# A recurrent attention kernel: the mask matmul cut to the columns of the last keys, the token-token mask moved to a multiply on GpSimd

## The chip, the cores and the metric

The kernel runs on one core of a Trainium2 chip. The metric is the device time of one execution in microseconds; a kernel is timed several times, alternating with the kernel before on the same chip, and medians of its runs are given. Engines are named as the profile names them: PE (TensorE), DVE (VectorE), ACT (ScalarE), POOL (GpSimd).

## The reference, cut to what matters

A memory-augmented attention walks over a sequence of 2048 tokens in 64 segments of 32 tokens. Each segment's input is 8 memory rows and its 32 tokens; the output of the memory rows is the memory of the next segment, so the segments follow each other strictly. The result is mixed with an MLP by a gate.

```python
L = M + seg_len                                    # 8 + 32
mask = (idx[:, None] < M) | (idx[:, None] >= idx[None, :])   # memory rows see all, tokens are causal
for s in range(n_seg):                             # 64
    h = jnp.concatenate([mem, xs], axis=1)
    # q, k, v of 32 heads of 128
    scores = jnp.einsum('bhqe,bhke->bhqk', q, k) * scale
    scores = jnp.where(mask[None, None], scores, -1000000000.0)
    p = _softmax(scores, axis=-1)
    # o = p v, projected by Wo
    mem = o[:, :M, :].copy()
```

## The kernel before

One segment's scores stand in one PSUM bank as 8 groups of 56 columns (EW = 56). E holds their exponentials, R the reciprocals of the sums over the keys. Pm is E times R for the memory rows, on the path to the next segment; Px is the same for the tokens, and racc adds up R for a check against overflow. Keys are on the partitions. Columns 8 to 47 of a group are 24 + 8 tokens and 8 memory rows against the main keys; columns 0 to 7 and 48 to 55 are queries against the last 8 keys (LEFT) of several segments, which are computed ahead and need a selecting mask. The mask is put in first, as a matmul of an identity with a mask tile of 448 columns; the scores are added on top.

```python
def mask_mm():
    B = bank(7, [P, 512])
    S = B[:, 0:NG * EW].rearrange("p (i e) -> p i e", e=EW)
    nc.tensor.matmul(S, lhsT=ident[:], rhs=MkA[:].unsqueeze(2).to_broadcast([P, 4, 2, EW]),
                     start=True, stop=True, skip_group_check=True)
    return B, S
...
for s in range(nseg + 2):
    ...
    if si == 3 and T + 1 < NT:
        left_v_in(T + 1)              # POOL: copy VL, 128 x 1024
    if si == 3 and T + 2 < NT:
        x_left(T + 2)                 # POOL: copy GL
    if live:
        ...
        if s + 1 < nseg:
            prep_h(s + 1)             # POOL: copy part of hT
        if s >= 1:
            prep_q(s)                 # POOL: copy part of QT
            x_mul(s - 1)              # POOL: products Px, and racc += R
        flush(dve_q)
        ...                           # projections, scores into S
        nc.scalar.activation(out=E[:, :, 0:16], in_=S[:, :, 0:16], func=ACTF.Exp, ...)
        nc.scalar.activation(out=E[:, :, 16:EW], in_=S[:, :, 16:EW], func=ACTF.Exp, ...)
        sm = bank(nc_, [P, NG, 8])    # sums over the keys, for the memory rows
        nc.tensor.matmul(sm[:], lhsT=BO[:], rhs=E[:, :, 8:16], start=True, stop=False)
        nc.tensor.matmul(sm[:], lhsT=BO[:], rhs=E[:, :, 0:8], start=False, stop=True)
        run_fill(5 + (si == 3))       # PE: independent matmuls of other segments
        nc.vector.reciprocal(out=R[:, 0:8 * NG]..., in_=sm[:])
        nc.vector.tensor_tensor(out=Pm[:]..., in0=E[:, :, 0:16]..., in1=R[:, 0:8 * NG]..., op=ALU.mult)
        av(Um, 8, s, V, Pm, 8, 0, 0)  # PE: Pm times V
        nc.tensor.matmul(sr, lhsT=BO[:], rhs=E[:, :, 16:48], start=True, ...)   # sums for the tokens
        ...
```

Four segments make a tile T of 128 tokens, si is the number within it. The copies at the head of a segment are independent of what runs there, and POOL, which works in order, does them early: those written at the head of segment s run during segment s - 1.

## Time and profile before

| what | value | where from |
|---|---|---|
| time | 851.37 us | median of 3 runs, 849.81 to 851.44 |
| PE busy | 96% of the span | page, part 1 |
| recurrent loop | 120 to 838 us, 64 segments of 11.2 us | busy time by stretches |
| mask matmul in the chain | 0.29 us a segment | chain in order of time |
| Pm beside an idle POOL | 0.29 us | timeline |

The chain in order of time is read as a list of pieces: the start, the length, and the engine and line whose work was the last to end there. The timeline gives every engine's instructions, also those off the chain. In the loop one PE matmul stream fills nearly all the time, so the questions to ask of a change are what it takes from PE and what PE will wait for. The lines themselves are in the prediction.

### The profile page before, as it was taken

The page shows a single profiled execution, that of the slowest core. Times are in us where ns is not written, and L with a number is a line of the kernel's source. Part 1 is how long each engine was busy: PE and PEld are TensorE (multiplying, and loading weights), DVE is VectorE, ACT ScalarE, POOL GpSimd, SP SyncE. Part 2 cuts the span into 40 slices and gives each one's busy share as a digit, 9 for nine tenths or more (in the row PEclk, how much of TensorE's full clock was granted, in tenths as well). Part 3 has the DMA queues.
Part 4 walks back from the last instruction along what each step waited for, and adds up shares of the span by engine and source line. Part 5 has one row for each costly group of instructions (what it writes and reads, how often), then busy time and mean ns, then how long its engine had stood idle before and what let it go on. Part 6 is the DMA issues. An engine that isn't in the chain of part 4 may idle for free.

```text
span 848.8 us, 49249 instructions
## 1 busy us (share of the span) xinstructions
PE 813.2 (96%) x22417; PEld 495.7 (58%) x22417; DVE 502.4 (59%) x1017; ACT 434.2 (51%) x1244; POOL 275.2 (32%) x625
## 2 busy tenths in 40 slices
PE   4989999999999999999999999999999999999986
PEld 2655455566656666556666665656665666656554
DVE  4555335666665666565666566666656566657553
ACT  2444454555545554555455555555454545555552
POOL 8000123333233424242424342333324342424220
PEclk8999999999999999999999999999999999999999
DMA  9890221010101010101000000101010101010000
GB/s 317 268 361 8 65 63 27 4 35 4 35 10 35 4 34 12 34 12 30 15 22 24 19 26 17 29 10 35 10 35 7 34 9 36 9 31 9 10 4 24
DMA packets 38216, 37.64 MB, mean 44 GB/s; under 512 B 13545, under 2 KB 36434, under 8 KB 36466
## 3 DMA queue, kind: packets, MB, share of 16 engines
q1 hardware_dynamic: 37874, 34.31, 12.3%
q8 instruction: 177, 2.90, 1.4%
q14 instruction: 37, 0.30, 0.1%
q0 software_dynamic: 128, 0.13, 0.1%
HBM read 26.03 MB, written 6.29 MB: 38 GB/s over the span
## 4 chain that ended last, share of the span: by engine, by line
PE 90%; DVE 6%; issue 1%; DMA 1%; SPq 1%; ACT 1%; DVEq 0%; ACTq 0%
PE b L210 34%; PE b L232 17%; PE b L221 17%; PE b L383 5%; PE hp L454 3%; PE bp L471 3%; PE b L359 2%; PE b L368 2%; PE b L660 1%; PE b L695 1%; PE b L388 1%; PE b L649 1%; DVE st L401 1%; DVE junk L422 1%; DMA Wo_sb<-in_A_x_dram 1%
## 5 line engine op out<-in xcount | busy, mean ns | idle before, releaser
L216 DVE STREAM_TRANSPOSE Tt<-b 128x512 f32<-128x512 f32 (+1 forms) x384 | 225.6, 613 | 79.1 <-PE b L210 65.4
L210 PEld LDWEIGHTS <-hT 128*32 128x32 bf16 x5120 | 134.8, 97 | 100.0 <-DVE hT L696 15.7
L232 PE MATMUL b<-Wo_sb,UTT 128*32 128x256 bf16 (+1 forms) x4736 | 162.7, 285 | 1.2 <-ACT UTT L595 0.8
L221 PE MATMUL b<-Wv_sb,hT 128*32 128x512 bf16 x2048 | 141.9, 378 | 0.0
L210 PE MATMUL b<-Wq_sb,hT 128*32 128x512 bf16 x2048 | 133.0, 379 | 1.4 <-DVE hT L696 1.4
L210 PE MATMUL b<-Wk_sb,hT 128*32 128x256 bf16 (+1 forms) x3072 | 133.4, 308 | 0.0
L232 PEld LDWEIGHTS <-UTT 128*32 128x32 bf16 x4736 | 121.3, 97 | 19.6 <-ACT UTT L595 1.5
L630 ACT CAST KT<-Tt 128x256 bf16<-128x256 f32 (+1 forms) x192 | 87.1, 476 | 53.6 <-DVE Tt L216 53.5
L581 POOL TENSOR_TENSOR Px<-E,R 128x256 bf16<-128x256 bf16 x64 | 43.1, 673 | 219.0 <-DVE R L665 219.0
L665 DVE RECIPROCAL R<-b 128x256 f32<-128x256 f32 x64 | 112.5, 1757 | 0.0
L630 POOL CAST QT<-Tt 128x512 bf16<-128x512 f32 x64 | 39.3, 614 | 192.3 <-DVE Tt L216 192.3
L595 ACT CAST UTT<-b 128x256 bf16<-128x256 f32 x256 | 76.8, 386 | 23.6 <-PE b L388 23.1
L684 ACT CAST wsb<-b 128x256 bf16<-128x256 f32 x66 | 24.6, 373 | 120.0 <-PE b L232 120.0
L653 DVE RECIPROCAL R<-b 128x64 f32<-128x64 f32 x64 | 35.6, 557 | 79.1 <-PE b L650 79.1
L630 ACT CAST QT<-Tt 128x512 bf16<-128x512 f32 x64 | 39.6, 619 | 67.6 <-DVE Tt L216 67.6
L459 ACT ACTIVATE hg<-hp,b_sb 128x256 bf16<-128x256 f32 x80 | 37.6, 473 | 54.1 <-PE hp L454 54.1
L383 PEld LDWEIGHTS <-V 32*128 32x128 bf16 x4096 | 35.2, 91 | 46.5 <-DVE Pm L655 32.4
L221 PEld LDWEIGHTS <-hT 128*32 128x32 bf16 x2048 | 49.5, 96 | 21.1
L664 ACT CAST UTT<-b 128x64 bf16<-128x64 f32 x128 | 20.9, 215 | 75.6 <-PE b L388 75.6
L454 PE MATMUL hp<-yT,w_sb 128*128 128x256 bf16 (+1 forms) x352 | 55.8, 284 | 2.5 <-DVE yT L444 2.5
L583 POOL TENSOR_TENSOR racc<-racc,R 128x320 f32<-128x320 f32 x64 | 55.6, 868 | 0.0
L471 PE MATMUL bp<-w_sb,hg 128*128 128x512 bf16 x160 | 50.0, 392 | 3.7 <-DVE c_all L474 3.7
(116 smaller groups left out, 1046.5 us busy)
## 6 DMA issues: line engine op xcount, KB each, us to landing
Wv_sb<-in_A_Wv_dram SPq DMA_DIRECT2D x4, 1024.0 KB
Wq_sb<-in_A_Wq_dram SPq DMA_DIRECT2D x4, 1024.0 KB
Wk_sb<-in_A_Wk_dram SPq DMA_DIRECT2D x4, 1024.0 KB
Wo_sb<-in_A_Wo_dram SPq DMA_DIRECT2D x2, 2048.0 KB
vd<-vt SPq DMA_DIRECT2D x32, 128.0 KB
vs<-vd SPq DMA_DIRECT2D x256, 16.0 KB
out_dram<-o SPq DMA_DIRECT2D x16, 128.0 KB
Wo_sb<-in_A_x_dram SPq DMA_DIRECT2D x1, 1024.0 KB
```

What stands on the lines that cost most here:

```text
L210: nc.tensor.matmul(bk[32 * j:32 * j + 32, 0:n], lhsT=G[:, kc, :], rhs=W5[t][:, kc, h0:h1, j, :], start=(kc == 0), stop=(kc == KC - 1), til ...
L216: nc.vector.transpose(out=Tt[:, 0:n], in_=bk[:, 0:n])
L221: nc.tensor.matmul(bk[32 * j:32 * j + 32, :], lhsT=G[:, kc, :], rhs=Wv5[:, kc, 4 * vb:4 * vb + 4, j, :], start=(kc == 0), stop=(kc == KC - ...
L232: nc.tensor.matmul(bk[32 * g:32 * g + 32, :], lhsT=ut[:, i, j, c0:c0 + 32], rhs=Wo_sb[:, 4 * i + j, d0:d1], start=(j == 0 and i < 4), stop ...
L383: nc.tensor.matmul(U[j][:, i, :], lhsT=V[q, i, :], rhs=Pt[q, i, c_main:c_main + n], start=(i == 0), stop=False, skip_group_check=True, til ...
L454: nc.tensor.matmul(hp[:rows, :], lhsT=w1_sb[:, kc, fc * P:fc * P + rows], rhs=yTs[blk][:, kc, :], start=(kc == 0), stop=(kc == KC - 1))
L471: nc.tensor.matmul(bpt[T][:], lhsT=hg_[:rows, tt * P:(tt + 1) * P], rhs=w2_sb[:rows, fc, :], start=(fc == 0), stop=(fc == FC - 1))
L581: nc.gpsimd.tensor_tensor(out=Px[:, :, 0:32], in0=E[:, :, 16:48], in1=Rr, op=ALU.mult)
L583: nc.gpsimd.tensor_tensor(out=racc[:], in0=racc[:], in1=R[:], op=ALU.add)
L595: nc.scalar.copy(out=UTT[T % 2][:, :, j, c0 + M:c0 + 40], in_=U[:])
L630: (nc.gpsimd.tensor_copy if bi == 2 else nc.scalar.copy)(out=dst, in_=Tv)
L665: nc.vector.reciprocal(out=R[:, 8 * NG:].rearrange("p (i q) -> p i q", q=32), in_=sr)
```

## The change

The intent: 320 of the mask's 448 columns are a plain causal mask of tokens against tokens (or zero). They are left out of the matmul, and the exponentials that they would have made zero are multiplied by zero afterwards, on POOL, the engine with the most time to spare.

```diff
-    MkA = l0.tile([P, 4, EW], BF16)
+    MkL = l0.tile([P, NG, 2, LEFT], BF16)
+    Tri = l0.tile([P, RIDE], BF16)
...                                    (building the masks in the preamble, on POOL)
-        nc.tensor.matmul(S, lhsT=ident[:], rhs=MkA[:].unsqueeze(2).to_broadcast([P, 4, 2, EW]),
+        nc.tensor.matmul(S.rearrange("p i (a b) -> p i a b", b=LEFT)[:, :, 0:7:6, :], lhsT=ident[:], rhs=MkL[:],
                          start=True, stop=True, skip_group_check=True)
...
             nc.scalar.activation(out=E[:, :, 16:EW], in_=S[:, :, 16:EW], func=ACTF.Exp, ...)
+            Em = E[:, :, 16:16 + RIDE]
+            nc.gpsimd.tensor_tensor(out=Em, in0=Em, in1=Tri[:].unsqueeze(1).to_broadcast([P, NG, RIDE]), op=ALU.mult)
             sm = bank(nc_, [P, NG, 8])
```

More of the change, by code (lines that the diff above doesn't have):

```diff
@@ L152 @@
         nc.gpsimd.tensor_copy(out=SelL[i][:, RIDE:32], in_=Sel[:, LEFT * (SPT - 1 - i):LEFT * (SPT - i)])
-    nc.gpsimd.memset(MkA[:], 0.0)
-    for hh in range(4):
+    nc.gpsimd.memset(Tri[:], 1.0)
+    for g in range(4):
+        q = slice(32 * g, 32 * g + 32)
+        nc.gpsimd.affine_select(out=Tri[q, :], in_=Tri[q, :], pattern=[[1, RIDE]], compare_op=ALU.is_ge,
+                                fill=0.0, base=M, channel_multiplier=-1)
+    nc.gpsimd.memset(MkL[:], 0.0)
+    for i in range(0, NG, 2):
+        hh = i // 2
         for g in range(4):
             q = slice(32 * g, 32 * g + 32)
-            for (c0, c1) in ((0, M), (EW - LEFT, EW)):
-                sl = MkA[q, hh, c0:c1]
-                nc.gpsimd.affine_select(out=sl, in_=sl, pattern=[[0, c1 - c0]], compare_op=ALU.is_ge,
+            for c in range(2):
+                sl = MkL[q, i, c, :]
+                nc.gpsimd.affine_select(out=sl, in_=sl, pattern=[[0, LEFT]], compare_op=ALU.is_ge,
                                         fill=MASK_NEG, base=-LEFT * hh, channel_multiplier=1)
-            sl = MkA[q, hh, 0:M]
-            nc.gpsimd.affine_select(out=sl, in_=sl, pattern=[[0, M]], compare_op=ALU.is_ge,
+            sl = MkL[q, i, 0, :]
+            nc.gpsimd.affine_select(out=sl, in_=sl, pattern=[[0, LEFT]], compare_op=ALU.is_ge,
                                     fill=MASK_NEG, base=LEFT * hh + LEFT - 1, channel_multiplier=-1)
-            sl = MkA[q, hh, EW - LEFT:EW]
+            sl = MkL[q, i, 1, :]
             nc.gpsimd.affine_select(out=sl, in_=sl, pattern=[[1, LEFT]], compare_op=ALU.is_ge,
                                     fill=MASK_NEG, base=LEFT * hh, channel_multiplier=-1)
-            sl = MkA[q, hh, 2 * M:2 * M + RIDE]
-            nc.gpsimd.affine_select(out=sl, in_=sl, pattern=[[1, RIDE]], compare_op=ALU.is_ge,
-                                    fill=MASK_NEG, base=M, channel_multiplier=-1)
+        nc.gpsimd.tensor_copy(out=MkL[:, i + 1, :, :], in_=MkL[:, i, :, :])
     pools["nTt"] = 2
```

## The prediction

> **What bounds the kernel now.** I read the page first: the busy shares, the 40 slices, and the shares of the chain that ended last.
>
> ```profile
> PE 813.2 (96%) x22417; PEld 495.7 (58%) x22417; DVE 502.4 (59%) x1017; ACT 434.2 (51%) x1244; POOL 275.2 (32%) x625
> PE   4989999999999999999999999999999999999986
> PE 90%; DVE 6%; issue 1%; DMA 1%; SPq 1%; ACT 1%; DVEq 0%; ACTq 0%
> ```
>
> TensorE is busy in every slice but the first and the last ones, and 90% of the chain is its work. Busy time over four stretches says the same of the recurrent loop alone: from 120 to 838 us (64 segments, 11.2 us each) PE is busy 707.09 of 718 us. So time off PE is time off the kernel, as long as nothing new makes PE wait. Next, the chain in order of time, around the mask matmul of one segment (start, us, work):
>
> ```profile
> 402.42 0.14 PE b L649
> 404.15 0.22 PE b L660
> 404.73 1.75 PE b L232 x64
> 406.48 0.29 PE b L359
> 406.77 0.30 PE b L383 x32
> ```
>
> The mask matmul (L359) is on the chain, 0.29 us in each segment. Last, the timeline by engine, where the new Pool work must fit. Two segments, one of an ordinary sort, one of the sort that copies the last keys' values (VL) on Pool:
>
> ```profile
> 402.16 0.43 ACT L647 ACTIVATE E<-b 128x320 bf16<-128x320 f32 x1
> 402.48 0.20 ACT L647 ACTIVATION_READ_ACCUMULATOR E<-b 128x1 f32 x1
> 402.62 0.56 DVE L653 RECIPROCAL R<-b 128x64 f32<-128x64 f32 x1 [1.63 <-PE b L650]
> 403.28 0.29 DVE L655 TENSOR_TENSOR Pm<-E,R 128x128 bf16<-128x128 bf16 x1
> 403.71 0.36 PE L383 MATMUL b<-Pm,V 32*128 32x8 bf16 x32
> 404.09 0.28 PE L660 MATMUL b<-E,BO 128*128 128x256 bf16 x1
> ...
> 412.81 0.75 POOL L267 CAST KL<-Tt 128x256 bf16<-128x256 f32 x2 [0.81 <-DVE Tt L216]
> 413.47 0.20 ACT L647 ACTIVATION_READ_ACCUMULATOR E<-b 128x1 f32 x1
> 413.50 1.04 POOL L298 COPY VL<-vs 128x1024 bf16<-128x1024 bf16 x1
> 414.28 0.41 DVE L655 TENSOR_TENSOR Pm<-E,R 128x128 bf16<-128x128 bf16 x1
> ```
>
> The reader is to see two things. The second exponential is done at 402.68, and the sum that will need the masked exponentials (L660) starts at 404.09: a gap of 1.4 us. And Pm, which PE's next products (L383) need, takes 0.29 us beside an idle Pool but 0.41 us at 414.28, ending at 414.69, 0.15 us after Pool's VL copy (413.50 + 1.04 = 414.54). In another segment of that sort a copy that ended at 459.63 goes with a Pm of 0.68 us that ends at 459.78: again 0.15 us. Pm waits for Pool's instruction to end.
>
> **What the Trainium skill says.** Its page "SBUF — State Buffer", section "Who interferes with whom", says that a VectorE instruction with two SBUF inputs contends with a GpSimd instruction that reads SBUF, and that whichever starts first has the shared port for its whole instruction. Pm has two SBUF inputs (E and R), and the trace agrees: twice an end 0.15 us after Pool's. "TensorE: Matmul & The Clock Gate", section "Back-to-back issue gap", gives N/2.4 + 2.5 ns for N columns warm, 0.417 ns a column; the chain here gives 0.14 us for L649 (64 columns) and 0.22 for L660 (256), so 0.08/192 = 0.42 ns a column over a fixed 0.11 us. It agrees. "PSUM — Partial Sum Buffer", section "The four PSUM rules", says that a starting matmul clears the accumulate flags of its whole bank, and that later matmuls overwrite where the flag is clear: so the columns the mask no longer covers need no zeroing matmul. No run here shows that yet. "Perfetto Trace Analysis", section "GPSIMD Engine Instruction", says that a Pool row starts when its read is issued and ends when its write is acknowledged. In the trace a queued Pool instruction starts about 0.06 us before the end of the one before it (413.50 against 412.81 + 0.75 = 413.56).
>
> **The change part by part.** *Removed:* 320 of the 448 columns of L359, 64 times. By the slope 0.42 ns x 320 = 0.133 us each, and 0.29 - 0.133 = 0.16 us is left. 64 x 0.133 = 8.5 us, all on the chain. Its weight load, its wait for the reciprocal that reads the same bank, and its place in the order are unchanged; the instruction lists of both kernels agree for PE, DVE and ACT but for the form of L359 and a wait for Pool at L660.
>
> After the shorter mask matmul come L383, L388 and then L695, which needs wsb from an ACT cast that ends at 406.90; L695's load now starts at 407.08. Moved up by 0.133 to 406.95 it still finds its data, just. I take off nothing.
>
> *Moved:* building the masks in the preamble is about as many small Pool instructions (some 80 before, 75 after), long before L359 first runs at 116 us: 0.
>
> *Added:* one Pool multiply of 8 x 24 = 192 elements per segment, in place on E. Its duration from Pool's own rows: L581 does 256 elements in 0.673 us, L582 64 in 0.307, so 0.0019 us an element over 0.185, and 192 take 0.55 us. 64 of them are 35 us on an engine 32% busy. It starts when the second exponential is out, 402.68 + 0.08 (the delay of L581 behind its reciprocal) = 402.76, and ends at 403.31; L660 at 404.09 has 0.8 us to spare. In the ordinary sort no wait from that.
>
> *Its neighbours on Pool:* in the order of instructions the multiply stands in front of the next segment's copies (hT 0.27 us, QT 0.40, and in one segment of four VL 1.04 and GL), which today run before or beside the exponentials. All that follow now wait for it and then start at about 403.31 - 0.06 = 403.25, just as Pm issues (403.28). This is a race for the shared port. Pm's data took the last 0.15 us of its 0.29, so it can ask for the port as late as about 403.4. I think Pool wins more often than not, say 7 in 10.
>
> If Pool wins, in ordinary segments Pm ends behind hT: 403.25 + 0.27 + 0.15 = 403.67 in place of 403.57. PE has fill work until 403.78, so only about 0.02 us of it shows: 48 x 0.02 = 1 us, and 0.6 us more in some six segments that have no fill. In the VL segments Pm ends behind VL. Counted from the second exponential's start (413.15) VL would start at 1.09, end at 2.13, and Pm end at 2.28 us; today it ends at 1.54. That is 0.74 us, with PE at Pm's heels already, in 14 segments: 10.4 us, and about 0.5 in the one at 459 that already waits.
>
> Sum if Pool wins: 851.4 - 8.5 + 1.6 + 10.9 = 855.4 us. If Pm wins: 851.4 - 8.5 = 842.9 us, or a little less.
>
> **The rivals.** (1) *The clean gain*, 843 us: the multiply hides, Pm gets the port between the multiply and the copy. For it: pending requests win today (GL, queued at 414.49, is the one that waits, 0.35 us in place of 0.30). Against: Pm issues some 0.03 us or more too late by my times. (2) *A new wait of Pm behind VL*, 855 us, as above: for it the 0.41 and 0.68 us; against it the thin margin of 0.03 to 0.1 us, on rows of Pool that are rough. (3) *L660 waits for Pool*: it would take another 0.8 us of delay, for which nothing in the trace speaks; by itself 64 x 0.2 us = 13 us if the multiply took 1.6 us. (4) *No gain from the mask matmul*, because its drain or the weight loads around it set the pace: 851 to 862. Against it: the column slope fits L649, L660 and L359 alike.
>
> **Range and chances.** 7 in 10 for about 855, 3 in 10 for about 843, with mixtures where some segments win and others lose. I put down 853, and a range of 841 to 859. Two per cent is 17 us: the gain can't exceed 8.5, so faster by over 2% gets 0.02; slower by over 2% needs more than my worst sum, 0.04; the rest is same.
>
> **What would show it.** The mask matmul at 0.16 us in the chain in place of 0.29 shows the saving. The Pool multiply at 0.5 to 0.6 us, starting 0.08 us after the exponential's accumulator read, shows the cost. Pm's duration decides: 0.29 us everywhere means the clean gain; about 1.1 us in the VL segments, with PE idle before L383 for 0.7 us, means the second. L660 must show no wait for Pool. I am wrong if the multiply takes over 0.8 us, if the mask matmul's chain share hardly falls, or if a copy delayed on Pool (QT, hT) stops PE later.

## The result, and the profile after

The changed kernel takes 854.69 us (median of 4 runs, 854.25 to 855.49), the kernel before in the same rounds 851.4 us. The ratio is 1.0039, with a 95% interval of 1.0019 to 1.006: 3 us slower, clear of noise, though within 2%. Ratios here and below are the mean time of one kernel's fast runs over the mean of the other's fast runs of the same rounds, so they are not quite the ratio of the medians quoted.

Three lines of the page of the changed kernel: busy shares, the shares of the chain by engine, and the new multiply.

```profile
PE 805.0 (94%) x22404; PEld 496.5 (58%) x22417; DVE 515.0 (60%) x1017; ACT 434.3 (51%) x1244; POOL 308.2 (36%) x682
PE 89%; DVE 7%; issue 1%; DMA 1%; SPq 1%; ACT 1%; DVEq 0%; ACTq 0%
L655 POOL TENSOR_TENSOR E<-E,Tri 128x192 bf16<-128x192 bf16 x64 | 35.2, 550 | 67.9 <-ACT E L653 67.9
```

PE has 8 us less work in a span 4.5 us longer. POOL has the 35.2 us of the multiply on top, 0.550 us each. DVE, whose instructions are the same, is 12.6 us busier: something stretches a DVE instruction. The chain in order of time, in a segment of the sort that copies VL and at the mask matmul after it:

```profile
415.13 0.04 PE b L658
415.17 0.02 issue
415.20 0.57 DVE R L661
...
415.86 1.16 DVE Pm L663
417.02 0.05 issue
417.07 0.36 PE b L389 x32
...
419.83 0.16 PE b L365
420.00 0.31 PE b L389 x32
```

The mask matmul (now L365) is 0.16 us where it was 0.29. But Pm (L663), which was not in the chain of such a segment before, is in it with 1.16 us, and PE's products L389 wait for it. The timeline of the changed kernel shows beside what it ran, first in an ordinary segment, then in that one (here and below only the lines that bear on the argument, most of them POOL's and DVE's):

```profile
404.46 0.55 POOL L655 TENSOR_TENSOR E<-E,Tri 128x192 bf16<-128x192 bf16 x1 [1.77 <-ACT E L653]
404.96 0.26 POOL L355 COPY hT<-xT 128x96 bf16<-128x96 bf16 x1
404.99 0.37 DVE L663 TENSOR_TENSOR Pm<-E,R 128x128 bf16<-128x128 bf16 x1
...
415.33 0.55 POOL L655 TENSOR_TENSOR E<-E,Tri 128x192 bf16<-128x192 bf16 x1 [0.20 <-ACT E L653]
415.83 1.04 POOL L304 COPY VL<-vs 128x1024 bf16<-128x1024 bf16 x1
415.86 1.15 DVE L663 TENSOR_TENSOR Pm<-E,R 128x128 bf16<-128x128 bf16 x1
417.07 0.36 PE L389 MATMUL b<-Pm,V 32*128 32x8 bf16 x32 [0.71 <-DVE Pm L663]
```

POOL's next instruction starts 0.05 us before the multiply is over, and 0.03 us before Pm. Pm then lasts until 0.14 us after the end of that instruction: 404.96 + 0.26 = 405.22 against 405.36, and 415.83 + 1.04 = 416.87 against 417.01. Behind the short hT copy this is nearly hidden by PE's fill work (the independent matmuls that run_fill puts there); behind the long VL copy PE stands for 0.71 us. In the totals of PE's waits, the kernel before and then the changed one (microseconds, times, longest):

```profile
PE b L383 <- DVE Pm L655: 5.9, 7, 1.3
```

```profile
PE b L389 <- DVE Pm L663: 14.7, 18, 1.3
```

Of the 15 segments that copy VL in the loop, 12 have a Pm of 1.15 us, and 3 have one of 0.29 us. In the 3, VL happened to start later than Pm; here is one, from the timeline of the changed kernel:

```profile
506.45 0.29 DVE L663 TENSOR_TENSOR Pm<-E,R 128x128 bf16<-128x128 bf16 x1
506.47 1.17 POOL L304 COPY VL<-vs 128x1024 bf16<-128x1024 bf16 x1
```

Two hundredths of a microsecond decide who waits: here POOL does, with 1.17 us for a copy of 1.04.

### The profile page after: what moved, and what is told of

Read it like the earlier page. It is cut to its first block, busy times and chain, and to the rows that moved or that the text cites. A ratio compares the mean times of both kernels' runs of the same rounds, so it can differ in the third digit from the quotient of the medians.

```text
span 853.3 us, 49323 instructions
## 1 busy us (share of the span) xinstructions
PE 805.0 (94%) x22404; PEld 496.5 (58%) x22417; DVE 515.0 (60%) x1017; ACT 434.3 (51%) x1244; POOL 308.2 (36%) x682
## 4 chain that ended last, share of the span: by engine, by line
PE 89%; DVE 7%; issue 1%; DMA 1%; SPq 1%; ACT 1%; DVEq 0%; ACTq 0%
PE b L216 32%; PE b L238 17%; PE b L227 16%; PE b L389 5%; PE hp L460 4%; PE bp L477 3%; DVE Pm L663 2%; PE b L374 2%; PE b L668 1%; PE b L703 1%; PE b L394 1%; PE b L365 1%; DVE R L661 1%; PE b L657 1%; DMA Wo_sb<-in_A_x_dram 1%
## 5 line engine op out<-in xcount | busy, mean ns | idle before, releaser
L389 PEld LDWEIGHTS <-V 32*128 32x128 bf16 x4096 | 35.7, 91 | 47.8 <-DVE Pm L663 41.6
L655 POOL TENSOR_TENSOR E<-E,Tri 128x192 bf16<-128x192 bf16 x64 | 35.2, 550 | 67.9 <-ACT E L653 67.9
```

Of the source, the lines that this page charges most:

```text
L389: nc.tensor.matmul(U[j][:, i, :], lhsT=V[q, i, :], rhs=Pt[q, i, c_main:c_main + n], start=(i == 0), stop=False, skip_group_check=True, til ...
```

## The experiments

Theory: the shorter mask matmul saves what it should; the multiply itself hides; but it pushes POOL's copies to the very moment at which Pm needs the SBUF port that DVE and POOL share, and Pm loses the race. Rivals: the saving is smaller than thought; the multiply holds PE by itself (its duration or its semaphore); Pm waits for POOL for a reason other than the port. The runs were made in three groups; each ratio is against the kernel before in the same rounds. "Loop" is the time from the first Pm's start to the last one's in the profiled execution, 63 segments, which leaves out a preamble that varies (the first Pm starts between 122.99 and 125.58 us); it is 706.16 us in the kernel before (123.09 to 829.25) and 709.24 in the changed one (123.66 to 832.90).

| run | median us | ratio (95% interval) | loop us |
|---|---|---|---|
| mask_only | 844.7 | 0.993 (0.9912 to 0.9948) | 699.45 |
| mul_only | 862.73 | 1.0143 (1.0125 to 1.016) | 718.18 |
| vl_late | 846.62 | 0.9963 (0.9944 to 0.9982) | 699.60 |
| mul_twice | 843.86 | 0.9926 (0.9907 to 0.9946) | 698.83 |
| pm_psum | 842.47 | 0.9896 (0.9881 to 0.9912) | 698.56 |
| all_late | 843.86 | 0.9914 (0.9901 to 0.9928) | 698.54 |
| before_late | 850.27 | 0.9988 (0.9974 to 1.0001) | 705.52 |
| pool_gap | 842.78 | 0.9908 (0.9891 to 0.9924) | 697.80 |
| junk_mul | 859.01 | 1.0094 (1.0073 to 1.0114) | 714.49 |

The medians of the kernel before in the three groups were 850.19, 851.02 and 850.7 us. All nine results passed the comparison with the reference.

**One half at a time.** mask_only leaves the multiply out, and is wrong:

```diff
-            Em = E[:, :, 16:16 + RIDE]
-            nc.gpsimd.tensor_tensor(out=Em, in0=Em, in1=Tri[:]..., op=ALU.mult)
```

> Only the short mask matmul, without the Pool multiply; wrong on purpose, as the token-token mask is then missing. If the saving is what the column slope says (0.133 us in each of 64 segments), 843 us (842 to 844), ratio to before 0.990. If the weight load or the drain around the mask matmul sets the pace, the rival, 850 to 851 us, ratio 0.999 or more.

Measured 844.7 us: a saving of 5.5 us by the medians, of 6.7 in the loop. That is the theory's side, but a little above the range, and less than the 8.5 expected. It passed the comparison although the causal mask is missing, so the comparison does not see this mask, and no "passed" here vouches for it; that the multiply puts it back is read from the code. Nor does it prove that the uncovered columns start afresh without a zeroing matmul, as the prediction has it.

mul_only has the mask matmul and mask tile of before, and the multiply:

```diff
+            Em = E[:, :, 16:16 + RIDE]
+            nc.gpsimd.tensor_tensor(out=Em, in0=Em, in1=Tri[:]..., op=ALU.mult)
```

> The full mask matmul as before, plus the Pool multiply (right result: the masked exponentials are zero already). Port theory: it pays the whole wait of Pm behind Pool and saves nothing, so 851.4 + 11 to 12.5 = 862.5 to 864 us, with Pm at about 1.15 us in 15 segments. Rival, the multiply costs nothing and the change merely fails to save: 851 to 852 us.

Measured 862.73, 12.5 us more than before: all of the loss belongs to the multiply. Pm is 1.15 or 1.16 us long in 14 of its 15 VL segments too.

**Which neighbour.** vl_late moves the VL copy on POOL, and nothing else:

```diff
-        if si == 3 and T + 1 < NT:
-            left_v_in(T + 1)
...
                 x_mul(s - 1)
+            if si == 3 and T + 1 < NT:
+                left_v_in(T + 1)
             flush(dve_q)
```

> The changed kernel with one edit: the copy of VL stands on Pool behind the products and the racc addition of the same segment, not straight behind the multiply. Port theory: in those 15 segments Pm then waits for the 0.30 us copy of GL at most, PE hardly waits before its products, 844 to 845.5 us, and Pm is nowhere longer than 0.5 us. Rival, the multiply itself (its reads, or its semaphore) holds Pm or PE: the time stays at 853 to 855 us and Pm stays long in the same segments.

Measured 846.62 us, a little above the range given, far from the rival's. Pm is 0.40 or 0.41 us in 13 of the 15 VL segments, now behind the GL copy, 0.37 or 0.38 in the ordinary ones behind hT, and nowhere over 0.51. The multiply still runs in every segment, so it isn't the multiply by itself that holds PE.

all_late moves the three other copies as well, so that nothing follows the multiply on POOL until the products:

```diff
-        if si == 3 and T + 1 < NT:
-            left_v_in(T + 1)
-        if si == 3 and T + 2 < NT:
-            x_left(T + 2)
...
-            if s + 1 < nseg:
-                prep_h(s + 1)
             if s >= 1:
-                prep_q(s)
                 x_mul(s - 1)
             flush(dve_q)
+            if s >= 1:
+                prep_q(s)
+            if s + 1 < nseg:
+                prep_h(s + 1)
+            if si == 3 and T + 1 < NT:
+                left_v_in(T + 1)
+            if si == 3 and T + 2 < NT:
+                x_left(T + 2)
```

> The changed kernel with all of Pool's copies of the segment (QT, hT, VL, GL) behind the products and the racc addition, so that nothing follows the multiply on Pool for some 2.5 us. Port theory: Pm is 0.29 us in nearly all segments, no PE wait before its products but in the few segments without fill, 842 to 843 us, ratio to before 0.989 to 0.990. If the later copies of QT or hT stop PE or hold VectorE's transposes, it is 845 us or more and the waits of PE name them.

Measured 843.86 us, a little above the range and below the rival's. Pm is 0.29 us in all 64 segments, and PE's waits for it are back where they were:

```profile
PE b L389 <- DVE Pm L664: 5.7, 6, 1.3
```

PE has no new wait for QT, hT or VL. But the later hT copy does hold DVE's transposes: they waited for it 16.0 us in all, 13 times (2.5 us, twice, in the control that follows; in the changed kernel not at all). None of that appears among PE's waits, so it came out of DVE's slack. This version beats both kernels by an order that leaves Pm no neighbour. The control, before_late, makes the same moves in the kernel before:

> The kernel before with the same reordering on Pool, as a control. Port theory: the only wait of Pm that it takes away is the 0.12 us of the VL segments and the 0.4 us of one of them, mostly hidden by fill work: 850.5 to 851.4 us, ratio 0.999 to 1.000. If the reordering is worth several us by itself, the gain of the reordered changed kernel is not the change's.

Measured 850.27 us, ratio 0.9988: Pm is 0.29 us in all segments there too, but it had little to win. So with the race out of the way in both, the change is worth 850.27 - 843.86 = 6.4 us, or 705.52 - 698.54 = 7.0 us in the loop. Segment by segment, by the starts of Pm, the saving is 0.13 us at the median, and 0.08 to 0.15 in 53 of the 63; the other ten together bring only 0.16 us, one of them being 0.38 longer. In the loop of all_late PE waits 2.5 us without a cause that the profile names ("issue"), in that of before_late 1.4.

**The port itself.** pm_psum keeps the order of the changed kernel but takes one of Pm's two inputs from PSUM in place of SBUF:

```diff
-            nc.vector.reciprocal(out=R[:, 0:8 * NG]..., in_=sm[:])
+            nc.vector.reciprocal(out=sm[:], in_=sm[:])
...
-                                    in1=R[:, 0:8 * NG]..., op=ALU.mult)
+                                    in1=sm[:].unsqueeze(2).to_broadcast([P, NG, 2, 8]), op=ALU.mult)
...
-        nc.gpsimd.tensor_tensor(out=racc[:], in0=racc[:], in1=R[:], op=ALU.add)
+        nc.gpsimd.tensor_tensor(out=racc[:, 8 * NG:], in0=racc[:, 8 * NG:], in1=R[:, 8 * NG:], op=ALU.add)
```

> The changed kernel, order of instructions as it is, but the reciprocal of the small sums stays in the accumulator memory and Pm reads it there, so that Pm has one input in the SBUF in place of two (the overflow sum then leaves out these reciprocals; the result is the same). Port theory: Pm no longer needs the shared port, takes 0.3 to 0.4 us in all segments though VL still runs beside it, and the time is 843 to 845 us. Rival, Pm waits for Pool for another reason (a semaphore, or plain SBUF bandwidth): Pm stays at about 1.15 us in 15 segments and the time at 854 to 855.

Measured 842.47 us, just below the range, and Pm is 0.29 us in all 64 segments. The timeline of a VL segment of this run:

```profile
412.19 1.04 POOL L304 COPY VL<-vs 128x1024 bf16<-128x1024 bf16 x1
412.23 0.29 DVE L663 TENSOR_TENSOR Pm<-E,b 128x128 bf16<-128x128 bf16 x1
```

VL starts 0.04 us ahead of Pm, as in the changed kernel, and neither waits: 0.29 and 1.04 us. The order and POOL's copies are the same; the second SBUF input is gone. So it is that input that waits. (The reciprocal now also writes to PSUM. POOL's addition to racc is shorter here, and the overflow check it feeds leaves these reciprocals out; this is an experiment, not a version to keep.)

**How close the race is.** mul_twice does the masked multiply twice in a row:

```diff
             nc.gpsimd.tensor_tensor(out=Em, in0=Em, in1=Tri[:]..., op=ALU.mult)
+            nc.gpsimd.tensor_tensor(out=Em, in0=Em, in1=Tri[:]..., op=ALU.mult)
```

> The changed kernel with the Pool multiply done twice in a row (zeros and ones, so the result is the same). Port theory: the second multiply now stands where the copies stood, so Pm ends behind it (about 1.8 us after the second exponential's start, in every segment) and then goes before VL: PE waits some 0.2 us in each of about 60 segments (12 us) but the 0.7 us in the 14 VL segments shrink to 0.2 too, so 855 to 859 us, and no Pm is longer than about 0.8 us. Rival, Pool's own time is on the path: 64 x 0.5 us more, about 885 us. Rival, Pm waits only where VL is and always for it: at least 0.5 us more in each VL segment, about 862 us, with Pm at 1.6 us there.

A miss: I expected 855 to 859, and it came out at 843.86, 11 us faster than the changed kernel with half a microsecond more of POOL work in each segment. Its timeline tells why:

```profile
410.87 0.55 POOL L655 TENSOR_TENSOR E<-E,Tri 128x192 bf16<-128x192 bf16 x1 [0.19 <-ACT E L653]
411.39 0.29 DVE L664 TENSOR_TENSOR Pm<-E,R 128x128 bf16<-128x128 bf16 x1
411.50 0.59 POOL L656 TENSOR_TENSOR E<-E,Tri 128x192 bf16<-128x192 bf16 x1
```

The second multiply starts at 411.50, 0.08 us after the first ends (411.42), not 0.05 us before; it is 0.07 to 0.09 us after in all 64 segments. In that gap Pm gets the port. The profile names no cause for the gap; the guess is that the second multiply waits for the first one's result, which it reads. To test this, junk_mul makes the second multiply independent of the first (it reads and writes other tiles):

```diff
+            nc.gpsimd.tensor_tensor(out=Gap[:], in0=Tri[:]..., in1=Tri[:]..., op=ALU.mult)
```

> The changed kernel with a second multiply of the same size that does not depend on the first (it multiplies the mask by itself into an unused tile). The run with the masked multiply twice came out at 844, not at the 855 to 859 expected, and the reason given for it is that its second multiply had to wait for the first one's result, so that Pm got the port in between. If that is right, an independent second multiply starts some 0.05 us before the first one's end, as a queued one does, wins the port, and Pm ends behind it in all segments, at 0.6 to 0.7 us long: 854 to 859 us. If the dependence has nothing to do with it: 843 to 845 us.

Measured 859.01 us, at the edge of the range. The second multiply now starts 0.03 to 0.05 us before the first one's end in all 64 segments, and Pm is 0.63 or 0.64 us in 59 of them:

```profile
417.42 0.51 POOL L657 TENSOR_TENSOR Gap<-Tri 128x192 bf16<-128x192 bf16 x1
417.44 0.64 DVE L665 TENSOR_TENSOR Pm<-E,R 128x128 bf16<-128x128 bf16 x1
```

Nearly the same work on POOL, 15 us apart, by whether its second instruction comes 0.02 us ahead of Pm or 0.11 behind. Last, pool_gap adds one tiny instruction to the changed kernel, a memset that only writes, to an unused tile:

```diff
+            nc.gpsimd.memset(Gap[:, 0, 0:8], 0.0)
```

> The changed kernel with one tiny write-only Pool instruction (a memset of 8 columns of an unused tile) between the multiply and the copies, which reads nothing from the SBUF and only makes the next copy start some 0.05 to 0.15 us later. The race theory: Pool lost the port to Pm wherever its copy started later than Pm (by 0.02 us in one case already) and won where it started 0.03 us earlier, so now Pm wins everywhere, is 0.29 us long, and the time is 843 to 845 us although Pool does more. Rival, the order alone decides (a copy standing next on Pool is always served first), or the delay is too small: 853 to 855 us with Pm at 1.15 us in the VL segments.

Measured 842.78 us, a hair under the range, 12 us faster than the changed kernel:

```profile
410.46 0.10 POOL L657 MEMSET Gap<- 128x8 bf16 x1
410.50 0.29 DVE L665 TENSOR_TENSOR Pm<-E,R 128x128 bf16<-128x128 bf16 x1
410.50 1.18 POOL L305 COPY VL<-vs 128x1024 bf16<-128x1024 bf16 x1
```

Started in the same hundredth of a microsecond, Pm now takes its 0.29 us and VL is the one that waits, with 1.18. The ten traces in which Pm has both inputs in SBUF agree, these and the two kernels' own: where a reading POOL instruction started 0.01 to 0.04 us ahead of Pm (236 times), Pm was longer than 0.29 us every time; where it started 0.00 to 0.03 us behind (66 times), Pm took 0.29 every time. The three repairs, pm_psum, all_late and pool_gap, have overlapping intervals; which of them is fastest stays open. all_late is the one that does not live on a margin of a few hundredths of a microsecond.

## Why the prediction was right

It put down 853 us with 94% on "within 2%", from 7 chances in 10 for about 855.4 and 3 for 842.9. Measured: 854.69, and, with the race decided the other way, 842 to 844. The range, 841 to 859, held both outcomes, so the total alone proves little; the mechanism is borne out by Pm's 1.15 us and PE's wait of 0.71.

- *The saving.* The chain shows 0.16 us for the mask matmul, as worked out. On the whole path it is a little less than the 8.5 us of the sum: 6.4 to 7.0 us between the two reordered kernels. From the end of the projection to the next segment's work the chain goes from 0.86 us (406.48 to 407.34) to 0.74 (408.19 to 408.93), and the median of all segments is 0.13: the term of one segment is right, and "I take off nothing" holds there. What is missing lies in the ten irregular segments; 1.1 us of it fits the longer "issue" waits (2.5 against 1.4 us), whose cause stays open. So 64 full savings were 1.5 to 2 us too many. The working rests on the slope of the column formula; the "It agrees" said of it holds for the slope alone, as the chain's fixed part is 0.11 us and the formula's 2.5 ns.
- *The multiply.* 0.550 us against 0.55; it starts 0.08 us behind the accumulator read (415.05 + 0.20 against 415.33). The sum over the tokens (now L668) waited for nothing in the changed kernel.
- *The race.* POOL won it in 12 of 15 VL segments and in 46 of the 49 others (not in the first two and the last), mostly by 0.03 or 0.04 us. The prediction thought Pm could ask as late as 0.1 us after its start; that was wrong, its start decides, as the 236 and 66 cases above show.
- *The cost of losing.* Pm in the VL segments 1.15 us (about 1.1 said), PE's wait 0.71 us (0.7 said), but in 12 segments, not 14: 9.0 us more of PE waiting for Pm than in the reordered kernel (14.7 - 5.7). In ordinary segments Pm ends 0.08 us later, not 0.10. In the loop the loss is 709.24 - 698.54 = 10.7 us, where the sum had 12.5. By the same pairing as above, a VL segment that lost the race is 0.78 us longer than in the reordered kernel at the median (9.2 us in 12 of them), an ordinary one 0.01. Saving and loss were both too large, by about 2 us each, and cancelled: that the total came within 1 us of the 855.4 is in part luck.
- *The rivals.* The clean gain was there for the taking; all_late measures most of it. A wait of the token sums for POOL did not occur, and the mask matmul's own saving was real.

## What to carry to other kernels

An instruction moved to an idle engine costs not only its own time: what is queued behind it moves too, and may land on the one moment when another engine needs a port that both share. Look, for each new instruction, at what its engine ran next and beside what that now falls; put long copies behind work that has slack (and see who then waits for them, as DVE's transposes did here), or take one of the two SBUF inputs of the instruction on the path from PSUM. A result that hangs on a few hundredths of a microsecond is best made independent of them by order.

## What the Trainium skill lacked or had wrong

- "SBUF — State Buffer", section "Who interferes with whom": right that the one that starts first keeps the port to the end of its instruction, and that one SBUF input does not contend (pm_psum, 0.29 and 1.04 us side by side). It lacks how near the decision is and what decides it in a trace: the starts shown. 0.02 to 0.03 us ahead, POOL made Pm wait 0.08 to 0.86 us; at the same start or 0.02 us behind, POOL itself took 0.13 to 0.14 us longer (1.17 and 1.18 against 1.04). And no page says by how much a queued POOL instruction starts before the end shown of the one ahead of it, here about 0.05 us (415.83 against 415.33 + 0.55), so that DVE found no gap to slip into.
- "GPSIMD Engine Reference", section "2.1 Instruction dispatch": it asks for a wait on the producer where a POOL instruction reads what another core wrote in the one before, but gives no cost of such a wait. Here a second multiply that reads the first one's result started 0.08 us after its end (411.50 against 411.42), an independent one 0.04 us before it (417.42 against 416.91 + 0.55).
